# Mixed spectrum stored mode-innermost, Y W in two blocks of 96 channels, channel weights fetched last, side items moved

## The chip, the cores and the metric

The kernel runs on one core of one Trainium2 chip. Its time is the device time of one execution in microseconds (us). A core has five engines with an instruction queue each: TensorE (PE, the matrix engine; its weight loads are listed as PEld), VectorE (DVE), ScalarE (ACT), GpSimd (POOL) and SyncE (SP). Here POOL issues all loads and four of the output DMAs, and SP issues the other output DMAs. Matmul results go to PSUM, which has eight banks of 2 KB per partition.

## The reference

The input x has shape 8 x 3264 x 192 (batch, sequence, channels). Two layers are computed:

```
w = softmax(weight, axis=-1)                       # 8 heads x 7 taps
x = causal 7-tap convolution of x, each head its own taps on 24 channels
X = rfft(x, axis=1)[:, :64]                        # 64 modes
Yr = einsum('bmd,mde->bme', Xr, w_r) - einsum('bmd,mde->bme', Xi, w_i)
Yi = einsum('bmd,mde->bme', Xr, w_i) + einsum('bmd,mde->bme', Xi, w_r)
y = irfft(Y, n=S, axis=1)
u = x + y
out = u + relu(u @ w_ch)                           # w_ch is 192 x 192
```

Since `u @ w_ch` is `x @ w_ch + irfft(Y @ w_ch)`, the kernel forms both Y and Y W (64 modes, complex) and transforms both back with the same tables.

## The kernel before, in words

The batches are taken in four pairs, called q = 0 to 3. Time is cut into 25 tiles of 128 positions and a half tile of 64. All of x, later convolved in place, stays on the chip in bf16 (`xall`).

**Load and convolution.** POOL issues 24 units of x (`load_unit`, two DMAs each, which turn f32 into bf16), and beside some units a small load from the table `beside`: the half tiles, and with `small(k)` (line 218) the channel weights w_ch. `small(0)` and `small(1)` bring w_ch into `wm` and `w1`, `small(2)` and `small(3)` bring it again, in another order of rows, into `wc`. On POOL, lines 246 to 251 set up identity columns beside w_ch in `wm` and `w1`. PE convolves each unit (`conv_step`), DVE and ACT copy it back, PE adds it to the spectrum (`dft_unit`), and free time goes to transposing the convolved x into `cc` (`c_bank`).

**Mix.** `load_w(g)` (line 421) loads the weights w_r and w_i of four modes, 16 groups in all, over eight buffers. `mix(g)` (line 430) multiplies a group when its weights are there, and frees the buffer for a later group. After every two groups `mix_copy` (ACT) and `mix_trans` (line 447) turn the result round: PE transposes it, in two pieces t = 0 and 1 of the channels, and DVE and ACT copy the pieces to `yet`. Before the change, `yet` is [piece, component and mode, batch], the batch innermost, and the pieces are the channels 0 to 127 and 64 to 191 (the overlap is multiplied by zero rows of `w1`).

**Inverse transform of one pair.** `zw_part(q, c, z)` (line 511) multiplies `yet` by `wm` and `w1` for component c and pair q: the columns of a result are [Y W, 192 columns; Y, 192 columns], as `wm` and `w1` hold [w_ch rows; identity]. `zw_copy` (line 518) scales it and stores it as bf16 in `zw`. The pair q = 0 is done ahead of the output stage, q = 1, 2 and 3 as "side items" in it.

**Output stage.** `items` is an ordered list. An item is a "duo" of two tiles of 128 positions x 2 batches, a side item (the number q), or the half tiles of all batches ("h"). There are four PSUM buffers of two banks each, used in turn (`za` 0 and 1, `zb` 2 and 3: item n uses buffer n % 4), and six output buffers in `arena` (`outs`, item n uses n % 6). For a duo, `c_part` (line 473) gives x W, `m_part(n, 0)` (line 491) adds the inverse transform of Y W, `relu` (ACT, line 534) follows in place, `m_part(n, 1)` adds that of Y, and `finish` (DVE, line 559, then an output DMA on SP) adds x. The loop at line 616 sets the order: `m_part(n, 0)`, `relu(n)`, then `c_part(n + 1)` or, if the next item is a side item, its `zw_part` and `zw_copy`, and then `m_part(n - 1, 1)` and `finish(n - 1)`. Each engine runs its own instructions in that order and waits by semaphores. The "h" item sends its output through four DMAs on POOL (line 548).

Of the kernel before, what the change touches and what calls it, by code (L numbers as in the profile page):

```python
# [9 lines left out]
ALU = mybir.AluOpType  # L10
# [3 lines left out]
BF16 = mybir.dt.bfloat16  # L14
# [5 lines left out]
def kernel(  # L20
# [9 lines left out]
    nc = tc.nc  # L30
    B, S, D = x.shape
    H, KK = weight.shape
    MODES = moe_w_r.shape[0]
# [3 lines left out]
    P = 128  # L37
    NQ = B // 2
    NF = S // P
    NT = NF + 1  # L40
    HALF = S - NF * P
# [11 lines left out]
    def sb(name, shape, dtype, **kw):  # L53
        return pool.tile([P] + shape, dtype, tag=name, name=name, **kw)
# [4 lines left out]
    NW = 4  # L59
# [7 lines left out]
    fsin = sb("fsin", [NT, P], BF16)  # L67
    tabs = (ftab, fsin)

    yet = sb("yet", [2, 2 * MODES, B], BF16)  # L70

    mixa = sb("mixa", [3 * 2 * B * MODES], BF16)
    xt = mixa[:, :].rearrange("p (j k m) -> p j k m", j=3, k=2 * B)
    zw = mixa[:, 0:4 * NQ * D].rearrange("p (q c t d) -> p q c t d", q=NQ, c=2, t=2)
    band = sb("band", [H, 2 * P], BF16)
    wm = sb("wm", [2 * D], BF16)
    w1 = sb("w1", [2 * D], BF16)
    wc = sb("wc", [3, D], BF16)
    ident = sb("ident", [P], BF16)
    perm = sb("perm", [P], BF16)  # L80
# [3 lines left out]
    ymix = xs  # L84
# [5 lines left out]
    def wbuf(g):  # L90
        return wts[g] if g < NW + NL else wts[(g - NW - NL) % NW]
# [42 lines left out]
    low = [pp.tile([P, 512], F32, tag=f"low{i}", name=f"low{i}") for i in range(4)]  # L134
# [51 lines left out]
    for g in range(4):  # L186
        dst, srcv = band[32 * g:32 * g + 32, :, 32 * g:32 * g + PW], pk3[32 * g:32 * g + 32, :, :]
# [29 lines left out]

    def small(k):
        if k < 2:
            w, r = ((wm, slice(0, P)), (w1, slice(P, D)))[k]  # L220
            nc.gpsimd.dma_start(out=w[P - (r.stop - r.start):P, 0:D], in_=moe_w_ch[r, :])
        else:
            nc.gpsimd.dma_start(out=wc[64 * (k - 2):64 * (k - 2) + 64, :, :],
                                in_=moe_w_ch.rearrange("(p j) d -> p j d", j=3))

    beside = {3: (load_half, 0, 0), 4: (load_half, 0, 1), 6: (load_half, 1, 0), 7: (load_half, 1, 1),
              12: (small, 0), 14: (small, 1), 16: (small, 2), 18: (small, 3)}

    def load_units(k0, k1):
        for k in range(k0, k1):  # L230
            load_unit(*units[k])
            if k in beside:
                f, *a = beside[k]
                f(*a)
# [4 lines left out]
                            base=0, pattern=[[-1, P]], channel_multiplier=1)  # L239
    nc.gpsimd.memset(perm[:], 0.0)  # L240
    nc.gpsimd.affine_select(out=perm[:, 0:64], in_=perm[:, 0:64], compare_op=ALU.not_equal, fill=-1.0,
                            base=-64, pattern=[[-1, 64]], channel_multiplier=1)
    nc.gpsimd.affine_select(out=perm[:, 64:128], in_=perm[:, 64:128], compare_op=ALU.not_equal, fill=1.0,
                            base=0, pattern=[[-1, 64]], channel_multiplier=1)
    load_units(5, 9)
    nc.gpsimd.memset(wm[:, D:2 * D], 0.0)
    nc.gpsimd.memset(w1[:], 0.0)
    nc.gpsimd.affine_select(out=wm[:, D:2 * D], in_=wm[:, D:2 * D], compare_op=ALU.not_equal,
                            fill=1.0, base=0, pattern=[[-1, D]], channel_multiplier=1)
    nc.gpsimd.affine_select(out=w1[64:P, D:2 * D], in_=w1[64:P, D:2 * D], compare_op=ALU.not_equal,  # L250
                            fill=1.0, base=P, pattern=[[-1, D]], channel_multiplier=1)
    nc.gpsimd.memset(ascale[:], 2.0 / S)
    nc.gpsimd.memset(ascale[0:1, :], 1.0 / S)
    nc.gpsimd.memset(ascale[64:65, :], 1.0 / S)
# [148 lines left out]
    for k, u in enumerate(units):  # L403
# [5 lines left out]
        if k:  # L409
            q, t0, n = units[k - 1]  # L410
# [8 lines left out]
    NG = MODES // 4  # L419

    def load_w(g):
        if g < NG:
            for half, src in ((0, moe_w_r), (1, moe_w_i)):
                nc.gpsimd.dma_start(out=wbuf(g)[64 * half:64 * half + 64, :, :, :],  # L424
                                    in_=src[4 * g:4 * g + 4, :, :].rearrange("m (p j) e -> p m j e", j=3))
# [4 lines left out]
    def mix(g):  # L430
        yp = low[(g // 2) % 2][:, D * (g % 2):D * (g % 2) + D]
        for j in range(3):
            for p4 in range(4):
                m = 4 * g + p4
                nc.tensor.matmul(yp[32 * p4:32 * p4 + 2 * B, :], xt[:, j, :, m],
                                 wbuf(g)[:, p4, j, :], start=(j == 0), stop=(j == 2),
                                 tile_position=(0, 32 * p4), skip_group_check=True)
        if g < NW:
            load_w(g + NW + NL)
        elif g >= NW + NL:  # L440
            load_w(g + NW)

    def mix_copy(d, gs=slice(0, 2)):
        nc.scalar.copy(out=ymix[d % 2][:, gs, :],  # L444
                       in_=low[d % 2][:, 0:2 * D].rearrange("p (g d) -> p g d", g=2)[:, gs, :])

    def mix_trans(d, gs=slice(0, 2)):
        ets = [low[2 + t][:, :].bitcast(BF16)[:, 0:2 * P].rearrange("p (g k) -> p g k", g=2) for t in range(2)]
        for t in range(2):
            for g in range(gs.start, gs.stop):  # L450
                nc.tensor.transpose(ets[t][:, g, :], ymix[d % 2][:, g, 64 * t:64 * t + P], ident[:])
        m = slice(8 * d + 4 * gs.start, 8 * d + 4 * gs.stop)
        for t in range(2):
            dst = yet[:, t, :, :].rearrange("p (c m) b -> p m c b", c=2)[:, m, :, :]
            srcv = ets[t][:, gs, :].rearrange("p g (q k) -> p (g q) k", q=4)[:, :, 0:16].rearrange(
                "p m (c b) -> p m c b", c=2)
            if t == 0:
                nc.vector.tensor_copy(out=dst, in_=srcv)
            else:
                nc.scalar.copy(out=dst, in_=srcv)  # L460
# [30 lines left out]
    def m_part(n, which):  # L491

        duo, zt = items[n]
        for c in range(2):
            end = which == 1 and c == 1
            if duo[0] == "h":
                for k in range(2):
                    for i, r in enumerate(ROWS):
                        h = ROWS[i ^ k]
                        nc.tensor.matmul(zt[h, k, 0:2 * D], tabs[c][r, NF, 0:HALF], zw[r, 2 * k:2 * k + 2, c, which, :],  # L500
                                         start=False, stop=end, skip_group_check=True,
                                         tile_position=(r.start, h.start))
                continue
            (q0, t0), (q1, t1) = duo[0], duo[-1]
            parts = [(0, 2, q0, t0)] if t0 == t1 and q0 != q1 else [(k, 1, q, t) for k, (q, t) in enumerate(duo)]
            for k, w, q, t in parts:
                for i, r in enumerate(ROWS):
                    nc.tensor.matmul(zt[:, i, D * k:D * (k + w)], tabs[c][r, t, :], zw[r, q:q + w, c, which, :],  # L508
                                     start=False, stop=end and k + w == len(duo), skip_group_check=True)

    def zw_part(q, c, z):

        for t, w in enumerate((wm, w1)):
            for i, r in enumerate(ROWS):
                nc.tensor.matmul(z[r, 0:2 * D], yet[:, t, MODES * c:MODES * c + MODES, 2 * q + i], w[:],
                                 start=(t == 0), stop=(t == 1), tile_position=(0, 64 * i), skip_group_check=True)

    def zw_copy(dst, src, act):
        if act:
            nc.scalar.activation(out=dst, in_=src, func=ACT.Copy, scale=ascale[:, 0:1])  # L520
        else:
            nc.vector.tensor_scalar(out=dst, in0=src, scalar1=ascale[:, 0:1], scalar2=None, op0=ALU.mult)
# [2 lines left out]
    duos += [((q, t), (q + 1, t)) for q in (0, 2) for t in range(0 if q else 4, NF)]  # L525

    duos[-1:] = [(u,) for u in duos[-1]]
    for k, item in ((2, 1), (15, 2), (21, 3), (23, ("h",))):
        duos.insert(k, item)

    def relu(n):
# [67 lines left out]
    mix_copy(NG // 2 - 1, slice(1, 2))  # L599
    c_part(0)  # L600
    mix_trans(NG // 2 - 1, slice(1, 2))
    for c in range(2):
        zw_part(0, c, low[2 * c])
    for w in range(2):
        for c in range(2):
            zw_copy(zw[:, 0, c, w, :], low[2 * c][:, D * w:D * w + D], c)
    c_part(1)
    low_stack.close()
    stack, pp = psum_pool("pz1", "right")
# [3 lines left out]
    def is_duo(n):  # L613
        return 0 <= n < N and isinstance(duos[n], tuple)

    for n in range(N + 1):
        if is_duo(n):
            m_part(n, 0)
            relu(n)
        if n + 1 < N and n > 0:  # L620
            if is_duo(n + 1):
                c_part(n + 1)
            else:
                q, zt = items[n + 1]
                for c in range(2):
                    zw_part(q, c, zt[:, c, :])
                zw_copy(zw[:, q, :, :, :].rearrange("p c t d -> p c (t d)"), zt[:, :, 0:2 * D], q > 1)
        if is_duo(n - 1):
            m_part(n - 1, 1)
            finish(n - 1)  # L630
# [30 lines left out]
```

## Time and profile before

The median of six runs is 181.65 us (181.14 to 182.21). The profiled execution took 181.76 us; its span, from the first instruction to the last, is 180.0 us.

| what | where read | value |
|---|---|---|
| span | page, head | 180.0 us |
| PE, DVE, ACT, POOL busy | page, part 1 | 147.8, 112.0, 98.4, 68.9 us |
| granted TensorE clock, mean | cores | 0.981 |
| loads run | DMA rows of the slices | to about 107 us |
| last group of mix starts | timeline, line 435 | 107.76 us |
| first output DMA | timeline, line 572 | 114.32 us |
| last output DMAs issued | timeline, line 557 | 174.21 us, two in 1.09 us |

The profile shows one execution. Lines such as L508 are lines of the kernel. In a timeline each row has its start, how long it took, the engine, the line, the operation, output and input, the shape and the count of merged instructions, and in brackets how long the engine had been idle and what ended that.

### The profile page before, as it was taken

The numbers are of one execution on the slowest core, as the hardware profiler recorded it, in microseconds if no ns is written. First come the engines' busy times: TensorE is split into PE (matmuls) and PEld (weight loads), VectorE is DVE, ScalarE is ACT, GpSimd is POOL, SyncE is SP. The second block draws the span as 40 slices with busy tenths as digits, with TensorE's granted clock in tenths as the row PEclk, the third lists the DMA queues.
The fourth block names the chain that finished last, engine by engine and source line by source line (L and its number), as shares of the span: only waits on it lengthen the run. The fifth ranks groups of instructions, "written<-read, shape, count | busy, mean of one in ns | idle before, by whom it ended". The sixth has DMA issues, their size and how long they took to land.

```text
span 180.0 us, 6296 instructions
## 1 busy us (share of the span) xinstructions
PE 147.8 (82%) x2736; PEld 109.2 (61%) x2736; DVE 112.0 (62%) x159; ACT 98.4 (55%) x134; POOL 68.9 (38%) x113
## 2 busy tenths in 40 slices
PE   0047889999999998798577579999999999999950
PEld 0033556666667565676365557888776778888830
DVE  1878474866866583435244352788766878888880
ACT  8076646544554635165435355466776665667730
POOL 7999998778875644444243000000000500000000
PEclk9999999999999999789999999999999999999996
DMA  4999999999999999999999940469988699999994
GB/s 51 152 180 188 190 190 190 190 191 194 189 191 192 203 207 207 205 206 207 206 206 206 207 83 4 139 220 365 352 300 296 186 321 368 363 356 354 347 366 159
DMA packets 62875, 40.17 MB, mean 223 GB/s; under 512 B 28800, under 2 KB 62784, under 8 KB 62848
## 3 DMA queue, kind: packets, MB, share of 16 engines
q0 software_dynamic: 36224, 20.08, 80.4%
q1 hardware_dynamic: 26624, 19.69, 32.5%
q8 instruction: 21, 0.34, 0.8%
q14 instruction: 6, 0.05, 0.1%
HBM read 39.40 MB, written 20.05 MB: 330 GB/s over the span
## 4 chain that ended last, share of the span: by engine, by line
DMA 39%; issue 23%; POOL 19%; PE 13%; DVE 2%; ACT 1%; POOLq 0%; DVEq 0%
POOL xall L145 13%; DMA xall<-in_x_dram 13%; DMA arena<-in_moe_w_i_dram 12%; DMA cc<-in_moe_w_i_dram 6%; DMA arena<-in_moe_w_r_dram 6%; PE zb L508 4%; PE za L508 3%; PE za L488 3%; PE zb L488 3%; DMA out_dram<-arena 2%; DVE arena L559 2%; POOL xall L215 1%; POOL out_dram L548 1%; POOL arena L424 1%; ACT xall L321 1%
## 5 line engine op out<-in xcount | busy, mean ns | idle before, releaser
L145 POOL DMA_DIRECT2D xall<-in_x_dram x48 | 38.5, 810 | 6.0 <-DMA xall<-in_x_dram 4.4
L303 PE MATMUL z<-xall,band 64*64 64x192 bf16 (+3 forms) x816 | 27.6, 264 | 14.6 <-ACT band L189 10.6
L323 DVE CAST xall<-z 128x768 bf16<-128x768 f32 (+1 forms) x24 | 24.5, 1022 | 14.4 <-PE z L303 13.5
L303 PEld LDWEIGHTS <-band 64*64 64x64 bf16 x816 | 18.4, 110 | 23.2 <-ACT band L189 10.9
L321 ACT CAST xall<-z 128x768 bf16<-128x768 f32 (+1 forms) x24 | 20.4, 851 | 21.0 <-PE z L303 17.9
L488 PEld LDWEIGHTS <-cc 64*128 64x128 bf16 x600 | 27.0, 94 | 6.8 <-issue 2.0
L559 DVE TENSOR_TENSOR arena<-za,xall 128x768 f32<-128x768 f32 x26 | 24.8, 957 | 6.3 <-ACT za L534 2.0
L534 ACT ACTIVATE za<-za 128x768 f32<-128x768 f32 (+1 forms) x27 | 21.0, 783 | 9.7 <-PE za L508 9.7
L559 DVE TENSOR_TENSOR arena<-zb,xall 128x768 f32<-128x768 f32 x23 | 22.0, 957 | 6.3 <-ACT zb L534 2.9
L534 ACT ACTIVATE zb<-zb 128x768 f32<-128x768 f32 (+1 forms) x25 | 19.6, 782 | 10.1 <-PE zb L508 8.6
L329 PE MATMUL low<-xall,ftab 128*128 128x384 bf16 x100 | 22.0, 348 | 0.0
L383 PEld LDWEIGHTS <-xall 128*128 128x128 bf16 x300 | 18.7, 105 | 3.1 <-issue 0.3
L358 DVE COPY cc<-r 128x1024 bf16<-128x1024 bf16 (+1 forms) x16 | 10.2, 671 | 14.3 <-ACT xs L444 6.8
L548 POOL DMA_DIRECT2D out_dram<-arena x4 | 2.4, 616 | 43.1 <-DVE arena L540 43.1
L488 PE MATMUL za<-wc,cc 64*128 64x192 bf16 x318 | 17.9, 243 | 0.7 <-DVE arena L559 0.7
L508 PE MATMUL za<-mixa,fsin 64*128 64x384 bf16 (+1 forms) x120 | 18.1, 304 | 0.0
L508 PE MATMUL za<-mixa,ftab 64*128 64x384 bf16 (+1 forms) x120 | 18.1, 304 | 0.0
L508 PE MATMUL zb<-mixa,ftab 64*128 64x384 bf16 (+1 forms) x100 | 16.1, 313 | 0.4 <-ACT zb L534 0.4
L508 PE MATMUL zb<-mixa,fsin 64*128 64x384 bf16 (+1 forms) x100 | 16.1, 313 | 0.0
L488 PE MATMUL zb<-wc,cc 64*128 64x192 bf16 x282 | 15.8, 243 | 0.0
L356 ACT COPY cc<-r 128x1024 bf16<-128x1024 bf16 (+1 forms) x9 | 8.9, 989 | 10.7 <-PE r L383 9.6
L508 PEld LDWEIGHTS <-ftab 64*128 64x128 bf16 x220 | 11.8, 94 | 3.9 <-issue 1.5
(108 smaller groups left out, 185.2 us busy)
## 6 DMA issues: line engine op xcount, KB each, us to landing
out_dram<-arena SPq DMA_DIRECT2D x45, 384.0 KB, 4.4
xall<-in_x_dram POOLq DMA_DIRECT2D x24, 192.0 KB, 6.9
xall<-in_x_dram POOLq DMA_DIRECT2D x16, 240.0 KB, 6.9
arena<-in_moe_w_r_dram POOLq DMA_DIRECT2D x12, 288.0 KB, 9.9
arena<-in_moe_w_i_dram POOLq DMA_DIRECT2D x12, 288.0 KB, 10.7
out_dram<-arena SPq DMA_DIRECT2D x10, 192.0 KB, 2.8
xall<-in_x_dram POOLq DMA_DIRECT2D x8, 144.0 KB, 6.4
cc<-in_moe_w_r_dram POOLq DMA_DIRECT2D x4, 288.0 KB, 11.2
```

The lines of the kernel that those rows point to most:

```text
L145: nc.gpsimd.dma_start(out=xall[:, s0:s0 + nf, i, :], in_=src)
L303: mm = nc.tensor.matmul(ov[c], band[r, h, c.start + shift + 64 * (r is UP and c is LO): c.start + shift + 64 * (r is UP and c is LO) + 64] ...
L321: nc.scalar.copy(out=dst, in_=srcv)
L323: nc.vector.tensor_copy(out=dst, in_=srcv)
L329: nc.tensor.matmul(xp, ftab[:, t, :], xall[:, slot(q, t), :, :], start=(t == 0), stop=False, skip_group_check=True)
L356: nc.scalar.copy(out=out, in_=in_)
L358: nc.vector.tensor_copy(out=out, in_=in_)
L383: nc.tensor.transpose(tp[:, P * k:P * k + P], src, ident[:])
L488: nc.tensor.matmul(zt[:, i, D * k:D * k + D], cc[r, q, 3 * t + j, :], wc[r, j, :], start=(k == 0 and j == 0), stop=False, skip_group_check ...
L508: nc.tensor.matmul(zt[:, i, D * k:D * (k + w)], tabs[c][r, t, :], zw[r, q:q + w, c, which, :], start=False, stop=end and k + w == len(duo) ...
L534: nc.scalar.activation(out=zt[:, :, 0:w], in_=zt[:, :, 0:w], func=ACT.Relu)
L559: nc.vector.tensor_tensor(out=o[:, :, :].rearrange("p k (i d) -> p i k d", i=2), in0=zt[:, :, 0:2 * D].rearrange("p i (k d) -> p i k d", k=2),
```

## The change

`yet` becomes [channel in its half, piece, batch, component, mode]: the mode is innermost, only 96 partitions are used, and the pieces are the channels 96 to 191 (t = 0) and 0 to 95 (t = 1). The result of `zw_part` is laid out as four quarters of 96 columns: [Y of channels 0 to 95; Y W, two quarters; Y of channels 96 to 191]. So `wm` is [w_ch rows 96 to 191; identity] and `w1` is [identity; w_ch rows 0 to 95], both 96 rows x 288 columns, and each multiplies 288 columns in place of 384. `m_part(n, 0)` reads the quarters 1 and 2, `m_part(n, 1)` the quarters 0 and 3, which don't lie side by side. `zw_copy` of a side item becomes two instructions, the quarters 1 and 2 on DVE and 0 and 3 on ACT; before it was one, on DVE for q = 1 and on ACT for q = 2 and 3. In the order of the instructions the one on ACT waits for the one on DVE. The two loads of `wc` go to the units 12 and 15 of x, the loads of `wm` and `w1` go behind the last group of mix weights. The side items move from the places 2, 15, 21 and 23 (that of "h") to 2, 8, 11 and 14.

```diff
-    yet = sb("yet", [2, 2 * MODES, B], BF16)
+    HD = D // 2
+    yet = sb("yet", [2, B, 2, MODES], BF16)
...
-    zw = mixa[:, 0:4 * NQ * D].rearrange("p (q c t d) -> p q c t d", q=NQ, c=2, t=2)
+    zw = mixa[:, 0:4 * NQ * D].rearrange("p (q c b e) -> p q c b e", q=NQ, c=2, b=4)
+    QUARTERS = (slice(1, 3), slice(0, 4, 3))
-    wm = sb("wm", [2 * D], BF16)
-    w1 = sb("w1", [2 * D], BF16)
+    wm = sb("wm", [3 * HD], BF16)
+    w1 = sb("w1", [3 * HD], BF16)
...
     def small(k):
         if k < 2:
-            w, r = ((wm, slice(0, P)), (w1, slice(P, D)))[k]
-            nc.gpsimd.dma_start(out=w[P - (r.stop - r.start):P, 0:D], in_=moe_w_ch[r, :])
+            w, c, r = ((wm, 0, slice(HD, D)), (w1, HD, slice(0, HD)))[k]
+            nc.gpsimd.dma_start(out=w[0:HD, c:c + D], in_=moe_w_ch[r, :])
...
-              12: (small, 0), 14: (small, 1), 16: (small, 2), 18: (small, 3)}
+              12: (small, 2), 15: (small, 3)}
...
-    nc.gpsimd.memset(wm[:, D:2 * D], 0.0)
-    nc.gpsimd.memset(w1[:], 0.0)
-    nc.gpsimd.affine_select(out=wm[:, D:2 * D], ..., pattern=[[-1, D]], channel_multiplier=1)
-    nc.gpsimd.affine_select(out=w1[64:P, D:2 * D], ..., pattern=[[-1, D]], channel_multiplier=1)
+    for w, c in ((wm, D), (w1, 0)):
+        nc.gpsimd.memset(w[0:HD, c:c + HD], 0.0)
+        nc.gpsimd.affine_select(out=w[0:HD, c:c + HD], ..., pattern=[[-1, HD]], channel_multiplier=1)
...
         elif g >= NW + NL:
             load_w(g + NW)
+            if g + NW == NG - 1:
+
+                small(0)
+                small(1)
...
-                nc.tensor.transpose(ets[t][:, g, :], ymix[d % 2][:, g, 64 * t:64 * t + P], ident[:])
+                nc.tensor.transpose(ets[t][0:HD, g, :], ymix[d % 2][:, g, HD - HD * t:D - HD * t], ident[:])
...
-            dst = yet[:, t, :, :].rearrange("p (c m) b -> p m c b", c=2)[:, m, :, :]
-            srcv = ets[t][:, gs, :].rearrange("p g (q k) -> p (g q) k", q=4)[:, :, 0:16].rearrange(
+            dst = yet[0:HD, t, :, :, m].rearrange("p b c m -> p m c b")
+            srcv = ets[t][0:HD, gs, :].rearrange("p g (q k) -> p (g q) k", q=4)[:, :, 0:16].rearrange(
...
-    nc.tensor.matmul(zt[:, i, D * k:D * (k + w)], tabs[c][r, t, :], zw[r, q:q + w, c, which, :],
+    nc.tensor.matmul(zt[:, i, D * k:D * (k + w)], tabs[c][r, t, :], zw[r, q:q + w, c, QUARTERS[which], :],
...
-                nc.tensor.matmul(z[r, 0:2 * D], yet[:, t, MODES * c:MODES * c + MODES, 2 * q + i], w[:],
+                nc.tensor.matmul(z[r, HD - HD * t:2 * D - HD * t], yet[0:HD, t, 2 * q + i, c, :], w[0:HD, :],
                                  start=(t == 0), stop=(t == 1), tile_position=(0, 64 * i), skip_group_check=True)
...
-    for k, item in ((2, 1), (15, 2), (21, 3), (23, ("h",))):
+    for k, item in ((2, 1), (8, 2), (11, 3), (14, ("h",))):
         duos.insert(k, item)
...
-    for w in range(2):
+    for w in QUARTERS:
         for c in range(2):
-            zw_copy(zw[:, 0, c, w, :], low[2 * c][:, D * w:D * w + D], c)
+            zw_copy(zw[:, 0, c, w, :], low[2 * c][:, 0:2 * D].rearrange("p (b e) -> p b e", b=4)[:, w, :], c)
...
-                zw_copy(zw[:, q, :, :, :].rearrange("p c t d -> p c (t d)"), zt[:, :, 0:2 * D], q > 1)
+                for act, w in enumerate(QUARTERS):
+                    zw_copy(zw[:, q, :, w, :], zt[:, :, 0:2 * D].rearrange("p c (b e) -> p c b e", b=4)[:, :, w, :],
+                            act)
```

## The prediction

> **What bounds the kernel now.** I read the page, then the waits, the chain, and the timeline around each step of the change.
>
> ```profile
> span 180.0 us, 6296 instructions
> ...
> DMA  4999999999999999999999940469988699999994
> ```
>
> Each digit is 4.5 us: the DMA engines are full from 4.5 us to about 104 us, nearly empty to 113 us, and full again in the output stage. So there are three stretches: a load stream, a hand-over, and an output stage. The timeline of the hand-over has these rows:
>
> ```profile
> 107.76 0.45 PE L435 MATMUL low<-arena,mixa 128*16 128x192 bf16 x12 [0.66 <-DMA arena<-in_moe_w_i_dram]
> ...
> 109.26 0.44 PE L515 MATMUL low<-wm,yet 128*64 128x384 bf16 x2 [0.23 <-DVE yet L458]
> 109.54 0.33 PE L515 MATMUL low<-w,yet 128*64 128x384 bf16 x2
> ...
> 111.38 0.44 PE L515 MATMUL zb<-wm,yet 128*64 128x384 bf16 x2
> ...
> 112.41 1.02 DVE L522 TENSOR_SCALAR mixa<-zb,ascale 128x768 bf16<-128x768 f32 x1 [1.66 <-PE zb L515]
> ...
> 113.34 1.81 DVE L559 TENSOR_TENSOR arena<-za,xall 128x768 f32<-128x768 f32 x2
> ...
> 114.34 0.67 PE L488 MATMUL za<-wc,cc 64*128 64x192 bf16 x12 [0.36 <-DVE arena L559]
> ```
>
> The last group of the mix waits for its DMA, so the load stream sets when the hand-over begins. In the hand-over the path goes through `zw_part` of q = 0 and of q = 1, then DVE: its copy of q = 1 (1.02 us) stands ahead of the first two adds, and PE waits for the first add (0.36 us). In the output stage PE sets the pace:
>
> ```profile
> 123.23 0.67 PE L488 MATMUL za<-wc,cc 64*128 64x192 bf16 x12
> ...
> 124.38 0.67 PE L488 MATMUL za<-wc,cc 64*128 64x192 bf16 x12
> ...
> 125.52 0.67 PE L488 MATMUL zb<-wc,cc 64*128 64x192 bf16 x12
> ...
> 126.78 0.44 PE L515 MATMUL zb<-wm,yet 128*64 128x384 bf16 x2
> ...
> 128.23 0.96 DVE L559 TENSOR_TENSOR arena<-za,xall 128x768 f32<-128x768 f32 x1 [0.66 <-PE za L508]
> ...
> 129.25 0.67 PE L488 MATMUL za<-wc,cc 64*128 64x192 bf16 x12
> ```
>
> `c_part` comes every 1.146 us with no wait. The item at 126.78 is the side item q = 2; `c_part` at 129.25 comes just behind the end of the add at 128.23 + 0.96 = 129.19, whose buffer it takes. Beside "h" there is one more wait:
>
> ```profile
> 147.06 0.96 DVE L559 TENSOR_TENSOR arena<-za,xall 128x768 f32<-128x768 f32 x1 [0.84 <-DMA out_dram<-arena]
> ...
> 148.07 0.67 PE L488 MATMUL za<-wc,cc 64*128 64x192 bf16 x12 [0.29 <-DVE arena L559]
> ```
>
> The add six items behind "h" waits until the four POOL DMAs of "h" have left its output buffer; `c_part` was due at 147.61 and starts at 148.07, so it costs 0.46 us. From there the chain of work is PE to 170.8, then the last adds and their DMAs.
>
> **The change part by part.** All times are against the profiled execution (181.76 us, span 180.0, 1.76 around it), which lies 0.11 above the median of 181.65.
>
> **1. Channel weights out of the load stream.** `wm` and `w1` are 48 and 24 KB (73,728 bytes as written), and between 20 and 40 us the stream moves 190 GB/s: 0.39 us. All that is behind them, the last mix group too, lands 0.39 us earlier, and mix 15 starts at 107.37. That holds because each group of mix before it also waits for its DMA, and POOL has up to eight loads outstanding. Bounds: 0 (if one slow DMA engine sets the end) and 0.5. I take -0.39. `wc` goes earlier by a few units and still lies ahead of the weights: 0. On POOL the four operations at 20.93 to 22.31 (0.31, 0.47, 0.39 and 0.35 us) become four on 96 x 96, about 0.2 us each by the rows of 128 x 64 (0.24) and 128 x 128 (0.20 to 0.25). The DMA share is 1.59 to 1.60 all through 20 to 23 us, so POOL isn't late there and this is worth 0.
>
> **2. Channel weights behind the mix weights.** This adds a wait: the first `zw_part` now needs `wm` and `w1`. POOL issues them after 97.6, has nothing else to do until "h", and they lie behind the last group, which ends at 107.37: 107.37 + 0.39 = 107.76. `zw_part` needs them at about 108.9, 1.1 us later. So 0. The bad end: the stream's tail is long,
>
> ```profile
> 104.00:106.00 2.00, 1.43 (x31) 1.13 (x29) 0.78 (x3) 1.50 (x3) 0.00 (x0) 1.00 0.70 119
> 106.00:108.00 2.00, 1.34 (x31) 0.99 (x28) 1.39 (x3) 0.91 (x2) 0.00 (x0) 1.00 0.11 18
> ```
>
> (last columns DMA share and GB/s: few engines still work behind 105). If the two loads came a whole such tail (3 us) behind the last group, `zw_part` would stall 3 - 1.5 = 1.5 us.
>
> **3. `yet`.** Its copies now step by 256 bytes from one element to the next. They took 0.22 us (DVE) and 0.27 us (ACT) for 128 elements, 0.19 and 0.21 for 64. All but the last pair lie in waits for the mix weights (0.6 to 2.1 us each). For the last, DVE's speed on an f32 source (384 elements in 0.549 us against 1024 bf16 in 0.69) suggests it loses its faster mode: about +0.03 us. The Trainium skill, "Advanced Engine Details and Errata", section "SBUF Cachelines", speaks against this step: accesses that each fall into another 16-byte line are slower. The weight load of `yet` with a step of 16 bytes (0.193 us) against that of `xall` with a step of 6 (0.122) agrees, a factor of 1.6; were the copies slowed as much, it would be +0.11 and the sum 0.08 us worse.
>
> **4. `zw_part` of 288 columns.** Four pairs of matmuls at 0.163 us (109.54, 109.70, 109.86 are such starts), now by columns 0.122: -0.16 us for each of the four sets. The weight loads don't bind before (0.193 each, yet pairs pace by columns), and become shorter. Bounds: 0 and -0.16. I take -0.16.
>
> **5. The copy of q = 1.** It is 1.02 us on DVE. Half of it is 0.61 (between 0.413 for 192 columns and 1.018 for 768). `zw_part` of q = 1 ends 0.29 earlier (0.13 carried over from the first set, 0.16 its own), so DVE copies from 112.12 to 112.73. `m_part(0, 1)` is done at about 112.5, so the first add starts at 112.73 in place of 113.34 and ends at 113.69; `c_part` at 114.34 moves to 113.74, the next from 115.21 to 114.57. ACT's half (0.58) waits for DVE's, runs from 112.78 to 113.36 and is done before the relu of item 3 is ready at 113.6. With steps 3 and 4 in it: -0.60.
>
> **6. Side items q = 2 and 3.** PE gains 0.16 in each, but DVE now has 0.61 where it had nothing, ahead of an add. Followed from `m_part` of the item before (t): DVE's copy from t + 1.26, the add due at t + 1.72 starts at t + 1.81 and ends at t + 2.77; the `c_part` that takes its buffer starts at t + 2.83, before at t + 2.91. So the first gains about 0.1. The second is three places on, and DVE comes free of it late: there my count gives two stalls of 0.2, where before the second had none. Together 0. Bounds: -0.32 (PE's alone) and +0.6 (each copy's 0.61 delays one add, half of it is PE's). What queues behind DVE's copy is an add, its output DMA on SP and the buffer that `c_part` waits for; behind ACT's a relu, due 1 us later.
>
> **7. `m_part(n, 1)` reading two runs of 96.** 51 duos, 0.33 us each, 16.7 us of PE. Before, runs are 192 long, and single tiles (192 columns in one run) and pairs (384 in two) pace alike, so a break costs nothing. The nearest row with shorter runs is the convolution, which reads 24 elements at a time:
>
> ```profile
> 41.14 1.09 PE L303 MATMUL z<-xall,band 64*64 64x192 bf16 x40 [0.16 <-ACT xall L321]
> ```
>
> 40 in about 1.02 us to the next operation is 25.5 ns each over four quadrants, against 20.5 by the pace of `c_part` (12 in 0.49 us over two halves); turns on the banks are in that. So 0 to 25%: 0 to +4.2 us. I take 0, since 96 is nearer to 192 in breaks per column than to 24.
>
> **8. "h" at place 14.** The same four DMAs and the same six items to the next use: the wait of 0.46 stays. Bounds: -0.46, and +1.15 (one item) if the items now in front of "h" leave a queue. Output DMA: a duo is 393 KB in 1.146 us, 343 GB/s, and the stretch from 150 to 156 moves 366. So PE, not the DMA, goes on setting the end.
>
> Sum: 181.76 - 0.39 - 0.60 = 180.77, and 0.11 lower against the median: 180.66.
>
> **Rivals.** *A, other side: strided reads.* If the broken read of `m_part(n, 1)` costs more than 6% of 16.7 us, the 1.0 us gained is gone; at the convolution's 25% the time is 184.9. Against it: the paces of 192 and 2 x 192 are alike. *B, late channel weights.* From 1.1 us late on, `zw_part` stalls and PE with it; at the bound of 1.5 us of stall the time is 182.2. For it: the long tail; against: `wm` and `w1` took 6.9 and 7.5 us to land in the stream, as their neighbours did. *C, the gain is given back in the output stage.* Side items at 8 and 11 and "h" at 14 crowd on DVE and on the POOL DMAs: with +0.6 from step 6, 181.3; with half an item more at "h", 181.8. For it: step 6's count leaves little room. *D, more than summed:* the 0.46 behind "h" goes, as 40 items instead of 30 follow it and the DMAs have fewer gaps ahead: 180.2, and with the side items' PE gain 179.9. *E, the split and new layout do nothing in the hand-over* and only step 1 counts: 181.3.
>
> **How the numbers follow.** The forecast (180.3 to 181.1) has 0.52, D 0.14, C and E 0.18 of which two thirds within 0.3%, A 0.08, B 0.08. A measurement can tell 0.3%, about 0.55 us, from no change: faster is below 181.1, slower above 182.2. Faster 0.68, same 0.18 (C, E and a small B), slower 0.14. The range goes from 179.7 (D, with a little of the load bound) to 182.4 (B with its bound, a tenth of A); what is left out is most of A and the end of C.
>
> **What would show it.** Step 1: mix 15 at about 107.4. Step 2: `zw_part` waits for DVE's `yet`, not a DMA. Step 4: its starts 0.12 apart. Step 5: the first output DMA at 113.3. Step 6: `c_part` stalls of some 0.2 behind the side items. Step 7: `c_part` still 1.146 apart, else A holds. Step 8: one wait of DVE for an output DMA six items behind "h".

## The result

The changed kernel takes 179.96 us (median of 21 executions, 178.80 to 181.31); the kernel before, 181.41 us (47 executions). The ratio, by which the two are compared, is 0.9926, 95% interval 0.9911 to 0.9940: 1.1 to 1.6 us faster (the two medians alone give 0.9920). The forecast was 180.7 (179.7 to 182.4) and faster with 0.68.

The page of the changed kernel, head and DMA row (a digit is 1/40 of the span):

```profile
span 178.4 us, 6302 instructions
...
DMA  4999999999999999999999980469779999999994
```

The three stretches are as before. The gap of the DMAs between load and output is still there, and the thin part of the output stage, where side items take PE, has moved forward. The timeline of the hand-over after the change:

```profile
107.12 0.46 PE L437 MATMUL low<-arena,mixa 128*16 128x192 bf16 x12 [0.72 <-DMA arena<-in_moe_w_i_dram]
...
108.40 0.44 DVE L464 COPY yet<-low 96x64 bf16<-96x64 bf16 x1 [1.44 <-PE low L457]
...
108.89 0.31 PE L521 MATMUL low<-wm,yet 96*64 96x288 bf16 x2 [0.48 <-DVE yet L464]
109.04 0.29 PE L521 MATMUL low<-w,yet 96*64 96x288 bf16 x2
109.16 0.29 PE L521 MATMUL low<-wm,yet 96*64 96x288 bf16 x2
...
110.76 0.31 PE L521 MATMUL zb<-wm,yet 96*64 96x288 bf16 x2
...
111.55 0.62 DVE L528 TENSOR_SCALAR mixa<-zb,ascale 128x384 bf16<-128x384 f32 x1 [1.33 <-PE zb L521]
...
112.08 1.81 DVE L565 TENSOR_TENSOR arena<-za,xall 128x768 f32<-128x768 f32 x2
...
113.06 5.95 SPq L578 DMA_DIRECT2D out_dram<-arena  x8
113.08 0.67 PE L494 MATMUL za<-wc,cc 64*128 64x192 bf16 x12
```

Mix 15 starts 0.64 us earlier (107.76 to 107.12). The first `zw_part` is only 0.37 earlier (109.26 to 108.89): the copy to `yet` has become slow, 0.44 us for 64 elements against 0.19, and PE waits 0.48 us for it. The four matmul pairs start 0.12 us apart. DVE's copy of q = 1 takes 0.62 us. `c_part` of item 4 starts 1.26 us earlier (114.34 to 113.08). The output stage after it:

```profile
116.24 0.68 PE L494 MATMUL zb<-wc,cc 64*128 64x192 bf16 x12
...
118.45 0.66 PE L494 MATMUL za<-wc,cc 64*128 64x192 bf16 x12
119.76 0.67 PE L494 MATMUL zb<-wc,cc 64*128 64x192 bf16 x12
...
133.63 0.66 PE L494 MATMUL zb<-wc,cc 64*128 64x192 bf16 x12
134.77 0.66 PE L494 MATMUL zb<-wc,cc 64*128 64x192 bf16 x12
135.19 1.82 DVE L565 TENSOR_TENSOR arena<-za,xall 128x768 f32<-128x768 f32 x2 [0.67 <-DMA out_dram<-arena]
136.20 0.67 PE L494 MATMUL za<-wc,cc 64*128 64x192 bf16 x12
```

`c_part` still comes every 1.14 to 1.15 us, so the broken reads of `m_part(n, 1)` cost nothing. The wait behind "h" remains: the add at 135.19, six items behind "h", waits for the output DMAs, and the `c_part` that takes this add's buffer was due at 135.92 and starts at 136.20, 0.28 us late (0.46 before). The last `c_part` starts 1.56 us earlier (171.92 to 170.36), and the span is 1.6 us shorter.

So in the two profiles 0.64 us come from the load stream, 0.62 from the hand-over and 0.3 from the output stage, 0.18 of that the wait behind "h". The experiments help to tell which of this is the change and which is scatter.

**A measure for the experiments.** The times of one kernel spread by about 1 us around the median, so most parts of this change can't be told apart by time. The intervals between instructions in the profiles repeat far better. For all profiles, worked out from the starts in the timelines:

- a: start of mix 15
- b: mix 15 to the first `zw_part`
- c: first `zw_part` to `c_part` of item 4
- d: `c_part` of item 7 to that of item 34. In all kernels this holds the same work, the side items 2 and 3 and "h" among it
- e: the part of d by which the `c_part` that waits for the add six items behind "h" came late (over 1.146)

| kernel | a | b | c | d | e | d - e | ratio to before, interval |
|---|---|---|---|---|---|---|---|
| before | 107.76 | 1.50 | 5.08 | 31.70 | 0.46 | 31.24 | |
| changed | 107.12 | 1.77 | 4.19 | 31.41 | 0.28 | 31.13 | 0.9926 (0.9911 to 0.9940) |
| after_again | 106.94 | 1.77 | 4.19 | 31.40 | 0.27 | 31.13 | 0.9931 (0.9902 to 0.9959) |
| loads_back | 107.16 | 1.78 | 4.19 | 31.16 | 0.04 | 31.12 | 0.9953 (0.9928 to 0.9978) |
| loads_alone | 107.21 | 1.51 | 5.08 | 31.58 | 0.33 | 31.25 | 0.9962 (0.9936 to 0.9987) |
| loads_fourfold | 109.00 | 1.78 | 4.19 | 31.40 | 0.27 | 31.13 | 1.0047 (1.0026 to 1.0068) |
| yet_back | 106.79 | 1.53 | 4.36 | 31.78 | 0.47 | 31.31 | 0.9950 (0.9930 to 0.9970) |
| split_back | 106.26 | 1.78 | 4.59 | 31.17 | 0.12 | 31.05 | 0.9968 (0.9946 to 0.9989) |
| places_back | 106.87 | 1.78 | 5.76 | 31.39 | 0.28 | 31.11 | 0.9963 (0.9941 to 0.9986) |
| modes_inner | 107.22 | 1.56 | 4.19 | 31.39 | 0.28 | 31.11 | 0.9905 (0.9876 to 0.9933) |
| inner_and_first_split | 107.27 | 1.56 | 4.19 | 31.44 | 0.40 | 31.04 | 0.9909 (0.9877 to 0.9941) |
| h_on_sp | 106.91 | 1.57 | 4.19 | 31.05 | 0.00 | 31.05 | 0.9941 (0.9918 to 0.9964) |

b, c and d - e agree to 0.02 us between kernels that are alike in that part; a scatters over 1.0 us among the nine profiles with the loads moved (without the fourfold), and e over 0.4 us. The 5.76 of places_back has a cause of its own, shown below.

### The profile page after: what moved, and what is told of

It reads as the page before. It is cut to its first block, busy times and chain, and to the rows that moved or that the text cites. A ratio compares the mean times of both kernels' runs of the same rounds, so it can differ in the third digit from the quotient of the medians.

```text
span 178.4 us, 6302 instructions
## 1 busy us (share of the span) xinstructions
PE 147.5 (83%) x2736; PEld 108.6 (61%) x2736; DVE 116.6 (65%) x161; ACT 101.9 (57%) x135; POOL 68.3 (38%) x113
## 4 chain that ended last, share of the span: by engine, by line
DMA 48%; PE 30%; POOL 11%; issue 4%; DVE 3%; DVEq 0%; POOLq 0%
DMA xall<-in_x_dram 21%; DMA arena<-in_moe_w_i_dram 18%; POOL xall L149 8%; PE za L514 8%; PE zb L514 7%; PE za L494 7%; DMA cc<-in_moe_w_i_dram 6%; PE zb L494 5%; DMA out_dram<-arena 2%; DVE arena L565 2%; POOL out_dram L554 1%; PE zb L521 1%; POOL arena L426 1%; DVE arena L546 1%; PE low L437 1%
## 5 line engine op out<-in xcount | busy, mean ns | idle before, releaser
L305 PE MATMUL z<-xall,band 64*64 64x192 bf16 (+3 forms) x816 | 27.9, 264 | 14.8 <-DVE band L195 10.7
```

What stands on the lines that cost most here:

```text
L305: mm = nc.tensor.matmul(ov[c], band[r, h, c.start + shift + 64 * (r is UP and c is LO): c.start + shift + 64 * (r is UP and c is LO) + 64] ...
```

## The experiments

**The whole again: after_again.** The changed kernel, unaltered, measured once more.

> The changed kernel unaltered, beside the others on this chip. Every theory: 1.0 to 1.6 us below the kernel before. It is run since the four kernels that each undo one part all came out 0.75 to 0.85 us below, which would make the parts worth more than the whole; if the whole comes out near 1.0 here, the parts' values in time are inside the scatter, and only the trace separates them.

Measured: ratio 0.9931. The whole stands, and b, c and d - e are those of the first profile. That the kernels which undo one part all came out at 0.9950 to 0.9968 is no sum of parts: their intervals are 0.4% to 0.5% wide, and they ran on another chip (6 in the record) than after_again (11), without the changed kernel beside them. So whether 0.995 is the part undone or the chip can't be told from the times, and I read these kernels by the table.

**The loads: loads_back, loads_alone, loads_fourfold.** loads_back puts the small loads where they were:

```diff
-              12: (small, 2), 15: (small, 3)}
+              12: (small, 0), 14: (small, 1), 16: (small, 2), 18: (small, 3)}
...
-            if g + NW == NG - 1:
-
-                small(0)
-                small(1)
```

> The changed kernel with the loads of the channel weights where they were before (wm, w1 and wc beside units 12, 14, 16 and 18 of x, nothing behind the mix weights). The changed kernel is 1.4 us below the kernel before. Theory (the 72 KB leave the stream, 0.39 us at 190 GB/s): this one is 1.0 us below the kernel before, and mix 15 starts about 0.4 us later than with the change. Rival (the 0.64 us by which mix 15 came earlier is scatter in how the slowest DMA engine ends, since the mix groups 8 to 12 landed no earlier): still 1.4 us below. Second rival (all of the 0.64 us is the loads'): 0.8 us below.

Measured: 0.9953, and mix 15 at 107.16, against 107.12 and 106.94 in the two profiles of the changed kernel. The time (0.4 to 1.3 us below the kernel before) fits the theory and the second rival alike, the profile leans to the first rival; neither decides, since a scatters from 106.26 to 107.27 over the nine profiles with the loads moved.

loads_alone is the same edit, the other way round, on the kernel before.

> The kernel before with only the loads moved (wc beside units 12 and 15 of x, wm and w1 behind the mix weights). Theory: 0.39 us less to load ahead of the mix weights, 0.4 us below the kernel before, and zw_part does not wait for a DMA. Rival (the end of the stream scatters by more than that and sets itself): no change, 0 to 0.2 us.

Measured: 0.9962 (0.9936 to 0.9987), that is 0.2 to 1.2 us faster, b and c as before. So the loads alone make the kernel faster. The rival allows 0 to 0.2 us and is only just outside the interval, so the next run asks the same with a larger dose.

loads_fourfold adds eight loads of 36 KB to the stream of the changed kernel:

```diff
+    def again(k):
+        nc.gpsimd.dma_start(out=wts[NW + NL - 1][0:HD, k // 3, k % 3, :], in_=moe_w_ch[HD * (k % 2):HD * (k % 2) + HD, :])
+
...
-              12: (small, 2), 15: (small, 3)}
+              12: (small, 2), 15: (small, 3),
+              9: (again, 0), 10: (again, 1), 11: (again, 2), 13: (again, 3),
+              14: (again, 4), 16: (again, 5), 17: (again, 6), 18: (again, 7)}
```

> The changed kernel with eight more loads of half the channel weights (36 KB each, 288 KB in all) beside the units 9 to 18 of x, written to a buffer that later mix weights overwrite; nothing reads them. Theory (each byte ahead of the mix weights costs its time in the stream, 190 GB/s): 295 KB are 1.55 us, so mix 15 starts at about 108.5 and the time is 1.55 us above the changed kernel, 0.2 to 0.4 us above the kernel before. Rival (the end of the stream is set by something else, and small loads hide beside it): no more than 0.3 us above the changed kernel, 1.0 us below the kernel before.

Measured: 1.0047, 2.1 us above after_again (0.0116 of 181.4; by the two intervals 1.4 to 2.8), and in the timeline of PE:

```profile
109.00 0.46 PE L442 MATMUL low<-arena,mixa 128*16 128x192 bf16 x12 [0.70 <-DMA arena<-in_moe_w_i_dram]
```

Mix 15 still waits for its DMA, at 109.00; the median of the nine profiles with the loads moved is 106.94, so it is 2.06 us late (1.7 to 2.7 by the scatter of the nine), and b, c and d - e haven't changed. The rival falls: loads ahead of the mix weights cost about their full time, and rather more than less. What goes beyond 1.55 can be seen in the stream: from 44 to 56 us it moves 183 GB/s, in the changed kernel 190 and in the kernel before 191, and from 30 to 44 us 188 against 191; together that is worth about 0.7 us. POOL, which takes 0.54 to 0.58 us to issue each small load, is busy for 10.7 of the 12 us from 44 to 56, in the changed kernel for 8.7. Whether these issues or the small loads themselves slow the stream wasn't separated; a stretch of half clock from 85 to 91 us in this profile does not, as the stream keeps 205 GB/s there. The kernel before, with only the two loads of `wm` and `w1` more, moves 191 GB/s from 20 to 60 us as the changed kernel does. So a quarter of the 2.06, 0.52 us, is no better price for the change's 72 KB than 0.39.

**The layout of yet: yet_back, modes_inner.** yet_back stores the batch innermost again:

```diff
-    yet = sb("yet", [2, B, 2, MODES], BF16)
+    yet = sb("yet", [2, 2 * MODES, B], BF16)
...
-            dst = yet[0:HD, t, :, :, m].rearrange("p b c m -> p m c b")
+            dst = yet[0:HD, t, :, :].rearrange("p (c m) b -> p m c b", c=2)[:, m, :, :]
...
-                nc.tensor.matmul(z[r, HD - HD * t:2 * D - HD * t], yet[0:HD, t, 2 * q + i, c, :], w[0:HD, :],
+                nc.tensor.matmul(z[r, HD - HD * t:2 * D - HD * t], yet[0:HD, t, MODES * c:MODES * c + MODES, 2 * q + i], w[0:HD, :],
```

> The changed kernel with yet stored batch-innermost again (still two pieces of 96 channels). Theory: the copies of the last group, 0.42 and 0.44 us with the change, go back to 0.19 and 0.22, the first zw_part starts 0.23 us earlier, and the weight loads of yet, 0.193 us against 0.109, stay hidden behind the matmuls: 1.6 us below the kernel before. Rival (the weight loads with a step of 16 bytes now bind, since a pair of matmuls is 0.122 us and not 0.163): each of the four sets costs up to 0.2 us more, and the time is 1.4 to 1.0 us below.

Measured: 0.9950. Both sides were partly right. b falls from 1.77 to 1.53, as the theory has it, but c rises by 0.17 and d - e by 0.18: 0.09 us for each of the four sets. The start of `zw_part` shows where (the timeline of PE in yet_back):

```profile
108.32 0.40 PE L521 MATMUL low<-wm,yet 96*64 96x288 bf16 x2 [0.22 <-DVE yet L464]
108.55 0.29 PE L521 MATMUL low<-w,yet 96*64 96x288 bf16 x2
108.68 0.29 PE L521 MATMUL low<-wm,yet 96*64 96x288 bf16 x2
```

The second pair comes 0.23 us behind the first, the third 0.13 behind the second; with the mode innermost it is 0.15 and 0.12. So the weight load of 0.193 us is hidden in all pairs but the first. The kernel before shows the same: 0.28 us from the first pair to the second, then 0.16. So the new layout gains at PE what it loses at the copies (0.35 against 0.24 us), and a little more.

modes_inner keeps the layout and turns the loops of the copies round:

```diff
-            dst = yet[0:HD, t, :, :, m].rearrange("p b c m -> p m c b")
+            dst = yet[0:HD, t, :, :, m].rearrange("p b c m -> p c b m")
...
-                "p m (c b) -> p m c b", c=2)
+                "p m (c b) -> p c b m", c=2)
```

> The changed kernel with the loops of the copies to yet turned round, so that they write 4 or 8 modes side by side (16 bytes) and step through the batches outside. Theory (the copies of 0.42 to 0.70 us are slow because each 2-byte element they write goes 256 bytes on): they go back to about 0.2 and 0.25 us, and the first zw_part starts 0.2 us earlier; the weight loads keep 0.109 us: 1.6 us below the kernel before. Rival (any step is slow, also on the side that reads, now 64 bytes in PSUM): the copies stay above 0.4 us, 1.3 us below.

Measured: 0.9905. The instructions that touch `yet`, listed by line with duration in ns as minimum, median and maximum; first the kernel before:

```profile
L515 PEld LDWEIGHTS <-yet x32: 192/193/218, 109.3 to 134.1; 128*64 128x64 bf16 x32
L458 DVE COPY yet<-low x9: 182/215/226, 77.2 to 109.0; 128x128 bf16<-128x128 bf16 x7, 128x64 bf16<-128x64 bf16 x2
```

Then the changed kernel:

```profile
L521 PEld LDWEIGHTS <-yet x32: 106/110/110, 108.9 to 121.0; 96*64 96x64 bf16 x32
L464 DVE COPY yet<-low x9: 421/704/726, 77.9 to 108.4; 96x128 bf16<-96x128 bf16 x7, 96x64 bf16<-96x64 bf16 x2
```

Then modes_inner:

```profile
L521 PEld LDWEIGHTS <-yet x32: 106/110/110, 108.8 to 120.8; 96*64 96x64 bf16 x32
L464 DVE COPY yet<-low x9: 210/278/288, 76.7 to 108.5; 96x128 bf16<-96x128 bf16 x7, 96x64 bf16<-96x64 bf16 x2
```

The copy falls from 0.42 to 0.21 us for 64 elements and from 0.70 to 0.28 for 128, and b from 1.77 to 1.56. What is slow is a write that steps 256 bytes from each element to the next; a read from PSUM that steps 64 bytes costs little (0.28 us for 128 elements, where yet_back, which writes and reads eight side by side, takes 0.21). The interval of the time overlaps that of the changed kernel, so the gain of 0.2 us is shown by the trace alone.

**The split copies: split_back.**

```diff
-                for act, w in enumerate(QUARTERS):
-                    zw_copy(zw[:, q, :, w, :], zt[:, :, 0:2 * D].rearrange("p c (b e) -> p c b e", b=4)[:, :, w, :],
-                            act)
+                zw_copy(zw[:, q, :, :, :].rearrange("p c b e -> p c (b e)"), zt[:, :, 0:2 * D], q > 1)
```

> The changed kernel with one copy per side item again, on DVE for q = 1 and on ACT for q = 2 and 3. Theory (DVE's copy ahead of the first two adds is on the path): it takes 1.02 us and not 0.62, the first output DMA leaves 0.4 us later; at the two other side items DVE is free and PE loses one stall of about 0.2 us less: 1.0 to 1.2 us below the kernel before. Rival (the split is worth nothing, since ACT's half waits for DVE's): 1.4 us below.

Measured: 0.9968. In its timeline DVE's copy is whole again and stands ahead of the adds, and PE waits for them as it did before the change:

```profile
110.70 1.02 DVE L528 TENSOR_SCALAR mixa<-zb,ascale 128x768 bf16<-128x768 f32 x1 [1.33 <-PE zb L521]
...
111.63 1.81 DVE L565 TENSOR_TENSOR arena<-za,xall 128x768 f32<-128x768 f32 x2
...
112.63 0.67 PE L494 MATMUL za<-wc,cc 64*128 64x192 bf16 x12 [0.36 <-DVE arena L565]
```

c is 4.59 against 4.19: the split is worth 0.40 us at q = 1. At q = 2 and 3 it costs 0.08 (d - e 31.13 against 31.05), which the adds explain: there it gives DVE, on which `c_part` waits, work that ACT had to itself.

**The places: places_back.**

```diff
-    for k, item in ((2, 1), (8, 2), (11, 3), (14, ("h",))):
+    for k, item in ((2, 1), (15, 2), (21, 3), (23, ("h",))):
```

> The changed kernel with the side items at 2, 15, 21 and 23 as before. Theory of the prediction (the places are worth nothing): 1.4 us below the kernel before, and the wait six items behind h as long as before, c_part 0.46 us late. Rival (more items behind h let the output DMAs catch up, and c_part is only 0.28 us late, as in the profile after): 1.1 us below.

Measured: 0.9963. d is 31.39, e 0.28, against 31.41 and 0.28: the places are worth nothing. Nor is the wait behind "h" shortened by more items after it: with the old places it is what it was with the new, and the 0.46 that the theory expected isn't there. Over all kernels that send "h" through POOL, e lies between 0.04 and 0.47 with no order. This profile took 181.73 us, 1.3 above its median; the windows of its hand-over (columns: the stretch and its length, busy us and instructions of PE, PEld, DVE, ACT and POOL, granted clock, DMA share, GB/s) show why:

```profile
108.00:110.00 2.00, 1.52 (x16) 0.88 (x17) 1.13 (x3) 0.70 (x2) 0.00 (x0) 0.72 0.03 8
110.00:112.00 2.00, 2.00 (x28) 1.63 (x26) 0.06 (x1) 1.00 (x3) 0.00 (x0) 0.50 0.00 0
112.00:114.00 2.00, 2.00 (x42) 1.71 (x42) 1.13 (x2) 1.44 (x3) 0.00 (x0) 0.93 0.00 0
```

The granted clock fell to 0.50 there, and c is 1.57 us longer. I come back to this at the end.

**A version from the findings: inner_and_first_split, h_on_sp.** The first is modes_inner with the copy split for q = 1 only:

```diff
-                for act, w in enumerate(QUARTERS):
-                    zw_copy(...)
+                if q > 1:
+                    zw_copy(zw[:, q, :, :, :].rearrange("p c b e -> p c (b e)"), zt[:, :, 0:2 * D], True)
+                else:
+                    for act, w in enumerate(QUARTERS):
+                        zw_copy(...)
```

> As modes_inner, and the copy is split over DVE and ACT only for q = 1, where DVE stands ahead of the first adds; for q = 2 and 3 ACT copies all. Theory: 0.2 us from the copies, and 0.08 us from the two side items, which is what split_back showed between c_part of items 7 and 17 (11.58 us against 11.66): 1.7 us below the kernel before. Rival (the first half of the output stage is not what sets the end): as modes_inner.

Measured: 0.9909, beside 0.9931 for the changed kernel (after_again); the intervals overlap. In the trace b is 1.56 and d - e 31.04, 0.21 and 0.09 us less: both gains are there, and too small to show in the times.

h_on_sp adds to it that "h" goes out through SP:

```diff
-                    nc.gpsimd.dma_start(out=dst, in_=o[r, k, :].rearrange("p (a d) -> p a d", a=2))
+                    nc.sync.dma_start(out=dst, in_=o[r, k, :].rearrange("p (a d) -> p a d", a=2))
```

> As inner_and_first_split, and the four output DMAs of the half tiles go through SP and not POOL. Theory (the add six items behind h waits only because POOL takes 0.61 us to issue each of the four and their DMAs move slowly): the wait of 0.3 to 0.8 us on DVE goes, c_part stays 1.146 us apart, 0.3 us below inner_and_first_split, 1.9 us below the kernel before. Rival (the four issues on SP hold up the output DMAs of the items behind h, which wait on the same queue): the wait moves to those, no gain or a loss of up to 0.5 us.

Measured: 0.9941, no gain. The wait is gone from PE's timeline:

```profile
134.29 0.66 PE L494 MATMUL zb<-wc,cc 64*128 64x192 bf16 x12
135.43 0.66 PE L494 MATMUL za<-wc,cc 64*128 64x192 bf16 x12
136.58 0.66 PE L494 MATMUL za<-wc,cc 64*128 64x192 bf16 x12
```

but the end hardly moved. SP's last issues (timeline of SP), first in inner_and_first_split, span 178.5:

```profile
172.63 1.12 SPq L563 DMA_DIRECT2D out_dram<-arena  x2
```

and in h_on_sp, span 178.3:

```profile
171.88 1.10 SPq L563 DMA_DIRECT2D out_dram<-arena  x2
```

They come 0.75 us earlier (0.36 of it because mix 15 is earlier, 0.40 by the wait), and the span is 0.2 us shorter. Neither side is right in full: the theory has the wait right and the gain wrong; the rival has the time right, but the wait didn't move to another item. The time went to the drain at the end: from the last issue to the end of the span it is 6.4 us here, and 5.4 to 6.2 in the other eleven profiles. In this profile the DMAs moved 367 to 368 GB/s in each 6 us from 134 to 158, a rate that the profile of before reaches only from 122 to 128 and, with its last outputs, from 170 to 176, and those of the changed kernel and of inner_and_first_split in no such stretch (363 and 364 at most). The pace of `c_part` asks for 343 GB/s (393 KB in 1.146 us). So PE and the output DMAs seem to be nearly level in this stage, so that a gain of PE inside it isn't a gain at the end. That last reading rests on one profile and wasn't tested further.

## Why the prediction was right, step by step

The direction and the range hold, and the sum was 0.3 to 0.4 us short: 1.0 forecast, 1.34 measured as a ratio (0.0074 of 181.4, interval 1.1 to 1.6). What the traces show of the parts is 0.62 in the hand-over and 0.11 at the side items; with 0.39 for the loads this makes 1.12, so the rest is not beyond scatter. The measured 179.96 us also falls where rival D put the time (179.9 to 180.2), but by chance: the wait that D counts on losing is still there.

- **Step 1 (loads, -0.39).** The mechanism is right: the fourfold loads cost 2.1 us in time and 2.06 at mix 15. The size is not settled: loads_alone gives 0.2 to 1.2 us, and a quarter of the fourfold loads 0.52, a part of which is the slower stream of that run alone. The 0.64 of the first two profiles is this and scatter.
- **Step 2 (no wait for the late weights).** Right: the first `zw_part` waits for DVE's copy in the profile after, and rival B didn't occur. `wm` and `w1` are issued at 97.65 and 98.73 there and take 9.6 and 8.7 us, so they are in at about 107.4, 1.5 us ahead of `zw_part`.
- **Step 3 (copies of yet, +0.03).** Wrong, the one term mis-sized by much: +0.27 (b 1.50 to 1.77). I took only the loss of DVE's fast mode from a row of f32. The Trainium skill, "Advanced Engine Details and Errata", section "SBUF Cachelines", which says that accesses falling each into another 16-byte line are slower, was the better guide here. Against the factor of 1.6 of the weight loads it was 2.3 for 64 elements and 3.3 for 128 on DVE, and 2.1 and 2.7 on ACT. modes_inner takes 0.21 of the 0.27 back.
- **Step 4 (288 columns, -0.16 a set).** The pace is as forecast, 0.12 us. "The weight loads don't bind before" was wrong for the first pair of each set: its 0.193 us lay open, which the rows at 109.26 and 109.54 already held (0.28 us, not 0.16), and the shorter load gains 0.09 more a set, as yet_back shows.
- **Step 5 (split of q = 1).** Right: forecast with steps 3 and 4 as -0.60, measured -0.62 (b + c from 6.58 to 5.96), and split_back gives 0.40 for the split alone, 1.02 less 0.62. That the sum is so near is luck in part: the rest of it, -0.62 + 0.40 = -0.22, is 0.27 lost at the copies and 0.49 gained at the two sets, where the working had 0.03 and 0.32. It also let the first add start when DVE's copy ends, while in both profiles the add starts 0.09 us before that (113.34 against 112.41 + 1.02, and 112.08 against 111.55 + 0.62). These three errors, 0.24, 0.17 and 0.09 us, nearly cancel.
- **Step 6 (side items, 0).** d - e fell by 0.11. The split costs 0.08 there and the shorter weight loads gain 0.18, against the 0 that I took from two opposite stalls. These two make 0.10 and leave nothing for the 0.16 a set that fewer columns save on PE. places_back has q = 2 where the kernel before has it, and shows why PE's gain there is not the stage's: the first `c_part` step over q = 2 is 2.21 us and not 2.45, but `c_part` then waits for DVE's adds, and the three steps together are 4.67 us, before 4.59. q = 3 wasn't followed in this way.
- **Step 7 (broken reads, 0).** Right, rival A falls: the pitch of `c_part` is unchanged. The matmuls of 384 columns in `m_part` take 323 ns each on average, as before.
- **Step 8 ("h", 0).** The wait stayed in kind. Its change of 0.18 us between the two profiles is scatter: e is 0.04 in loads_back, which has "h" at 14, and 0.28 in places_back, which has it at 23. D, which would have it vanish through the place, falls with the 0.28 and 0.27 that remain in the two profiles of the changed kernel. That the output DMAs don't set the end was thinner than the working had it, if h_on_sp is read rightly.
- **Rival E** (nothing in the hand-over) falls with c. **Rival C** didn't happen: the output stage gave nothing back (d - e fell).

## What to carry to other kernels

Where a stretch is a chain over several engines, price every instruction on it by the access pattern that it will have, the writes too: a copy of 64 elements doubled its time by stepping 256 bytes, and turning its loops round repaired that while the layout, and the faster weight load that it was made for, stayed. Bytes ahead of the load that the chain waits for cost about their full time here, so whatever is needed only at the end of the chain can go last. And before taking a stall out of the middle of a stage, look at whether the output DMAs behind it would have been able to deliver sooner.

## What was not expected of the hardware

In each of the profiles the granted TensorE clock falls to 0.50, once or twice while PE still has work, each time for about 3.4 us (in loads_fourfold once for 6.8), at places that no edit explains: around 73 to 79 us in before, the changed kernel, loads_back, yet_back, loads_alone, inner_and_first_split and h_on_sp, around 25 to 29 us in split_back and modes_inner, at both in after_again, around 85 to 91 us in loads_fourfold, and at 109 to 112 us in places_back. Most of these places lie in the load stream, where the DMAs set the pace, and what a dip costs there wasn't measured; in the hand-over, where PE is on the path, it cost 1.57 us. The Trainium skill, "TensorE: Matmul & The Clock Gate", section "Part 1: The HAM clock gate", ascribes a half-rate clock to a gate that watches how busy PE was over a window of about 3.4 us; the rate and the length fit, and PE is thinly used ahead of the dips (in before, busy for 1.3 of the 3 us from 71 to 74). But a whole idle window, which the page names as the condition, isn't in the traces: the longest gap of PE just ahead of a dip is 2.6 us (loads_fourfold), and ahead of the one in places_back no gap is over 1.0 us. What places the dip in a given execution stays open, and it may be a good part of the spread of the times.
